# A Fourier filter and a swish layer on one core: the first batch multiplied from 94-row stationaries with one table, its rotations, filter loads and last stage rearranged, and four a1 buffers

## The chip, the core and the metric

The kernel runs on one core of a Trainium2 chip. The core has TensorE (PE, matrix products, with weight loads PEld), VectorE (DVE), ScalarE (ACT), GpSimd (POOL) and SyncE (SP, which here only issues DMAs). The metric is the device time of one execution in microseconds, as a median of runs.

## The reference

A batch of 8 sequences, 3008 tokens of 256 features, goes through a filter in the frequency domain and then through two matrices with a swish between them:

```python
X = np.fft.rfft(x, axis=1)
F = (filt_r + 1j * filt_i)[None, :, :]
y = np.fft.irfft(X * F, n=x.shape[1], axis=1)
h = y.reshape(B * S, D) @ w_in                    # 256 -> 2048
out = (h * (1.0 / (1.0 + np.exp(-beta * h)))) @ w_out   # 2048 -> 256
```

## The kernel before

**The transform.** 3008 = 47 x 64, so each transform is two products with small tables: s1 (47 points), s2 (64 points, with twiddles, table `t2`), the filter, and back through s3 (table `t3`, from `t2` by transposes) and s4 (table `t4`, from `t1` by a transpose). 24 groups of frequencies (`NK`) are treated; filters lie in `fr_sb` and `fi_sb`.

**Two ways through it.** Batches 1 to 7 use `s1`, `s2`, `s3`, `s4` (lines 545 to 624): s1 takes 94 rows of x (47 x 2) with the table `t1`, evicts into tiles `a1`, which `a1_store` writes to DRAM (line 344) and `a2_load` reads back turned (line 558); the same happens between s3 and s4 (`z`, `zz`). Batch 0 has nothing to hide behind, so it has functions of its own (`s1_0`, `s2_0`, `s3_0`, `z_turn`, `s4_0`), which turn with TensorE transposes instead of DRAM. Units of that work are six: three parts of eight groups (`KH` = 8), for each half of the 256 features.

**The main loop.** 752 steps (47 blocks of 512 tokens x 16 blocks of the hidden 2048). A step makes two products into `hps` (line 704), ScalarE's Silu into `gT` (line 713), then whatever `plan` holds for this step, and the four products into `acc` of the step two before (line 724); after 16 steps `acc` is evicted to `ost` and stored. Pieces of the next batches' transforms are put at chosen steps by `at`; for batch 1, s2 pieces are at steps 17, 20, ..., 50, each s3 five steps later, odd s3 and s4 pieces evicted by ScalarE.

**What sets the order.** The schedule is manual: each engine executes its instructions in the order in which the program writes them. An instruction that waits holds all behind it on its engine. GpSimd's queue also issues the loads with a cast (x, filters of the upper half, w_in), SyncE's the others. In the compiled program the DMAs of GpSimd use eight semaphores in turn, those of SyncE eight others; a DMA that comes to a semaphore again first waits for the landing of the DMA that had it.

**The first batch in order** (lines 131 to 531). x is loaded as 47 rows of 64 points (`x0`), in five pieces of two DMAs each. `s1_0(g)` makes sixteen products with the table `t1d` into a tile of two PSUM banks, evicted into `aT`; `spin` makes products that nobody uses. `t3_part(g)` makes a third of `t3` by eight transposes. `t3_rotate` makes `t3s`, a copy of `t3` with halves exchanged and signs changed, on VectorE (line 323); group 0 of it comes from `c10` by a transpose (line 329). `a0_turn` transposes eight groups of `aT` into `a0`. `s2_0(n)` makes the products of unit n and VectorE multiplies them by both filters (line 428, two instructions `pq_t`); `s3_0(n)` adds the products with `t3` and `t3s` into one tile, evicted to `zT`. `z_turn(e, hh)` transposes to `zz0`, and `s4_0(e, hh)` makes eight points of the result into a two-bank tile, evicted and scaled into `y`. The loop can begin when all of `y` is written.

**PSUM in the first batch.** `spsum` has three tiles of two banks (s1, s2, s3, s4), `tpsum` two tiles of one bank (all transposes and `spin`).

**Filters.** Each filter comes in three parts (`parts`: groups 0 to 8 and 8 to 24 of the first 128 features, then all groups of the second), one DMA per part from SyncE for the lower rows and one from GpSimd for the upper. GpSimd then copies each unit's rows to the other half of the partitions (`spread`, lines 460 and 461). Between the spreads it issues the loads of w_in and of batch 1's x (`load_x`). `reciprocal` and `scale_wout` (line 369) prepare w_out, scaled by 1/beta.

Of the kernel before, what the change touches and what calls it, by code (L numbers as in the profile page):

```python
# [10 lines left out]
P = 128  # L11

ACT = mybir.ActivationFunctionType
ALU = mybir.AluOpType
# [7 lines left out]
N1 = 47  # L22
# [14 lines left out]
def kernel(  # L37
# [38 lines left out]
    apool = ctx.enter_context(tc.tile_pool(name="apool", bufs=2))  # L76
# [7 lines left out]
    def load_filters(eng, k0, k1, d0, d1):  # L84
        lo = eng is nc.sync
        n = k1 - k0
        for filt, dst, p0 in ((filt_r, fr_sb, 0), (filt_i, fi_sb, M)):
            q0, off, sg = (p0, k0, 1) if lo else (p0 + H, N1 - k0, -1)
            src = AP(filt.tensor, filt.offset + off * D + d0, [[N1 * D, H], [sg * D, n], [1, d1 - d0]])
            eng.dma_start(dst[q0 : q0 + H, k0:k1, d0:d1], src)  # L90

    parts = ((0, KH, 0, E2), (KH, NK, 0, E2), (0, NK, E2, D))
# [42 lines left out]
    def turn8():  # L135
        return tpsum.tile([P, KH, P], BF16, name="tps", tag="tps")
# [7 lines left out]
    def fold(t):  # L144
        nc.vector.tensor_scalar(
            t, t, 32 - BITS, 32 - BITS, ALU.logical_shift_left, ALU.arith_shift_right
        )

    t1d = sp.tile([N1, 2 * NK], BF16, name="t1d", tag="t1d")
# [8 lines left out]
    aT = sr.tile([P, NDC, 2 * NK, M], BF16, name="aT", tag="aT")  # L158
# [4 lines left out]
    x0 = sq.tile([N1, M, D], BF16, name="x0", tag="x0")  # L163
    xv0 = x[0].rearrange("(n m) d -> n m d", m=M)
# [4 lines left out]
    def load_x0(m0, m1):  # L169
        nc.gpsimd.dma_start(x0[:32, m0:m1, :], xv0[:32, m0:m1, :])  # L170
        nc.gpsimd.dma_start(x0[32:, m0:m1, :], xv0[32:, m0:m1, :])

    load_x0(0, 16)
# [3 lines left out]
    load_x0(16, 32)  # L177
    iota(vi[:, :, :H], [[1, NK], [N1, H]])
    load_x0(32, 48)
    iota(vi[:, :, H:], [[1, NK], [-N1, H]], base=N1 * (M - 1))  # L180
    load_x0(48, 56)
    load_x0(56, 64)
    load_filters(nc.gpsimd, *parts[0])
    make_identity(nc, ident)
    with nc.allow_non_contiguous_dma(reason="2048 values, once"):
        nc.sync.dma_start(beta_sb[:], moe_beta.rearrange("(fb fp) -> fp fb", fp=P))
    seen = sp.tile([1, 2], BF16, name="seen", tag="seen")
    nc.sync.dma_start(seen[:], x0[:1, 16, :2])
    for part in parts:
        load_filters(nc.sync, *part)  # L190
    for part in parts[1:]:
        load_filters(nc.gpsimd, *part)
# [9 lines left out]
    def affine(name, src, mul, add):  # L202
        t = small(name)
        nc.vector.tensor_scalar(t[:], src[:], mul, add, ALU.mult, ALU.add)
        return t

    pn = affine("pn", ip, TURN / N1, 0.0)
    nc.vector.tensor_scalar_mul(cc[:], cc[:], TURN / 4)
    kcf, ccf = (t[:].rearrange("p a b -> p (a b)") for t in (kc, cc))

    def phase47(name, scale):
        t = sq.tile([P, 2 * NK], I32, name=name, tag=name)
        nc.vector.scalar_tensor_tensor(t[:], kcf, scale[:], ccf, ALU.mult, ALU.add)
        fold(t[:])
        return t

    ph_d = phase47("ph_d", pn)
    nc.scalar.activation(t1d[:], ph_d[:N1], ACT.Sin, scale=TWO_PI / TURN)
# [3 lines left out]
    off = affine("off", c_i, -TURN / 4, TURN / 4)  # L222

# [20 lines left out]
    MG = 8  # L244
    aTv = aT[:].rearrange("p e k (g m) -> p g e k m", m=MG)

    def s1_0(g, engines):
        ps = bank2([P, NDC, 512])
        for e in range(NDC):
            for i in range(MG):  # L250
                nc.tensor.matmul(
                    ps[:, e, i * 2 * NK : (i + 1) * 2 * NK],
                    lhsT=x0[:, g * MG + i, e * P : (e + 1) * P],
                    rhs=t1d[:],
                    start=True,
                    stop=True,
                )
        src = ps[:, :, : MG * 2 * NK].rearrange("p e (m k) -> p e k m", k=2 * NK)
        if len(engines) == 1:
            evac(aTv[:, g], src, engines[0])  # L260
        else:
            for e in range(NDC):
                evac(aTv[:, g, e], src[:, e], engines[e])

    def spin(m, n):
        ps = tpsum.tile([P, 512], F32, name="tps", tag="tps")
        for i in range(n):
            nc.tensor.matmul(
                ps[:, : 2 * NK], lhsT=x0[:, m + i % 16, :P], rhs=t1d[:], start=True, stop=True
            )  # L270

    def a0_turn(kg, e, on_act):
        tp = turn8()
        for kk_ in range(KH):
            k2 = 2 * (kg * KH + kk_)
            nc.tensor.transpose(
                tp[:, kk_, :], aT[:, e, k2 : k2 + 2, :].rearrange("p c m -> p (c m)"), ident[:]
            )
        evac(a0[:, kg * KH : (kg + 1) * KH, e * P : (e + 1) * P], tp[:], on_act)
# [6 lines left out]

    t2_half(0)
    t2_half(1)
    s1_0(0, (False,))
    s1_0(1, (True,))  # L290
    spin(0, 26)
# [3 lines left out]
    n1s = affine("n1s", shift_and("n1_i", 1, M - 1), TURN / N1, 0.0)  # L295
    ph_t = phase47("ph_t", n1s)
    sn = sq.tile([P, 2 * NK], F32, name="sn", tag="sn")
    nc.scalar.activation(sn[:], ph_t[:], ACT.Sin, scale=TWO_PI / TURN)
# [4 lines left out]
    q_i = shift_and("q_i", 0, 1)  # L303
    q_p = (affine("q0", q_i, -1.0, 1.0), affine("q1", q_i, 1.0, 0.0))
# [3 lines left out]
    c10 = sp.tile([P, P], BF16, name="c10", tag="c10")  # L308
    s1_0(4, (False,))
    s1_0(5, (True,))  # L310
    t3_part(1, True)
    for c in range(2):
        nc.vector.tensor_copy(c10[:, c * M : (c + 1) * M], t2[:, 0, (1 - c) * M : (2 - c) * M])
    t1v = t1[:].rearrange("p (k q) -> p k q", q=2)
    for q in range(2):
        nc.vector.tensor_scalar_mul(t1v[:, :, q], sn[:NP], q_p[q][:NP])
    s1_0(6, (False,))
    t3_part(2, True)
    s1_0(7, (True, False))

    def t3_rotate(k0, k1):
        for c in range(2):
            nc.vector.tensor_scalar_mul(
                t3s[:, k0:k1, c * M : (c + 1) * M], t3[:, k0:k1, (1 - c) * M : (2 - c) * M], rot[c][:]
            )

    t3_rotate(1, KH)
    tp0 = turn8()
    nc.tensor.transpose(tp0[:, 0, :], c10[:], ident[:])
    nc.scalar.activation(t3s[:, 0, :], tp0[:, 0, :], ACT.Copy, scale=sgn[:])  # L330
# [132 lines left out]
    units = [(0, 0), (1, 0), (2, 0), (0, 1), (1, 1), (2, 1)]  # L463
    for e in range(NDC):
        nc.gpsimd.memset(zT[e][:, WZ:], 0.0)
    spread(0)
    spread(1)
    nc.gpsimd.dma_start(win_sb[:], moe_w_in.rearrange("(dc p) f -> p dc f", p=P))
    spread(2)
    load_x(1, 0)  # L470
    spread(3)
    load_x(1, 1)
    spread(4)
# [6 lines left out]
    def turn_t4():  # L480
        tp = turn8()
        nc.tensor.transpose(tp[:KP, 0, :NP], t1[:], ident[:NP, :NP])
        nc.scalar.activation(t4[:], tp[:KP, 0, :NP], ACT.Copy)
        nc.gpsimd.tensor_scalar(t4[0:4], t4[0:4], 0.5, None, ALU.mult)

    s2_0(0)
    s2_0(1)
    t3_rotate(KH, NK)
    a0_turn(2, 0, True)
    s3_0(0)  # L490
    s2_0(2)
    a0_turn(0, 1, True)
    turn_t4()
    s3_0(1)
    s2_0(3)
    a0_turn(1, 1, False)
    s3_0(2)
    s2_0(4)
    a0_turn(2, 1, False)
    z_turn(0, 0, True)  # L500
    z_turn(0, 1, True)
    s3_0(3)
    s2_0(5)
    s4_0(0, 0, True)
    z_turn(0, 2, True)
    s4_0(0, 1, True)
    s3_0(4)
    z_turn(0, 3, True)
    s4_0(0, 2, True)
# [5 lines left out]
    nc.vector.reciprocal(rbeta_sb[:], beta_sb[:])  # L515
    scale_wout(0)
    scale_wout(WG)
    s3_0(5, True)
    s4_0(0, 3, True)
# [4 lines left out]
    z_turn(1, 3, True)  # L524
    s4_0(1, 1, True)
    s4_0(1, 2, False)
    s4_0(1, 3, True)
# [112 lines left out]
    def s23_steps(b, steps, lag, act):  # L640
        assert len(steps) == NU
        for i, s in enumerate(steps):
            at(s, s2, b, i)
            at(s + lag, s3, b, i, act and i % 2 == 1)

    def s4_steps(b, steps, act):
        assert len(steps) == J // 4 * NDC
        for i, s in enumerate(steps):
            at(s, s4, b, i, act and i % 2 == 1)

    for b in range(1, B):
        o = first_step[b - 1]
        if b == 1:
            s1_steps(1, range(16), [o + i // 2 for i in range(16)], False, range(1, 16, 2))
            for g in range(NG):
                at(o + 10, a2_load, 1, g)
            s23_steps(1, [o + 17 + 3 * i for i in range(NU)], 5, True)
            for h in range(J // JG):
                at(o + 59, zz_load, 1, h)
            s4_steps(1, [o + 67 + (i * 12) // 15 for i in range(16)], True)  # L660
            for f in (2, 3):
                at(f, load_wout, f * WG)
                at(f, scale_wout, f * WG)
            if B > 2:
                for g in range(4):
                    at(o + 14 + 3 * g, load_x, 2, g)
                late = (54, 55, 56, 57, 58, 59, 60, 61, 66, 67, 68, 70, 72, 73, 74, 76)
                s1_steps(2, range(16), [o + r for r in late], False)
                for g in range(NG):
                    at(o + 80, a2_load, 2, g)  # L670
                if B > 3:
                    for g in range(4):
                        at(o + (62, 68, 88, 92)[g], load_x, 3, g)
            continue
# [98 lines left out]
```

## Time and profile before

| | |
|---|---|
| median of 7 runs | 799.27 us (797.0 to 803.3) |
| the profiled execution | 799.4 us, of which the span of the core is 797.4 us |
| granted TensorE clock, mean | 0.996 |
| first product of `s1_0` | 6.77 us after the span's start |
| first product of `s2_0` (line 423) | 21.33 us |
| first and last product by a filter on VectorE (line 428) | 22.44 us, 41.11 us |
| DMA engines' mean busy share, 4 to 44 us | about 1 in nearly every 2 us; 0.2 and below from 44 to 54 us |
| costliest groups | 3008 `acc` products 453.5 us, 752 Silu 516.5 us, 1636 `hps` products 428.3 us |

All times in the text are microseconds from the start of the span. A row of the timeline gives start, duration, engine, line, operation, output and inputs with their shape, how many instructions were merged, and in brackets the idle time of the engine before it and what ended it. A line can be that of a helper: line 112 is an eviction by ScalarE and lines 114 and 116 by VectorE, so that one goes by the names of the tiles. The kernel after has other line numbers.

### The profile page before, as it was taken

How to read it: one execution, taken by the hardware profiler on the slowest of the kernel's cores; microseconds unless marked ns; L12 is line 12 of the kernel's file. 1: busy time of each engine (PE TensorE's matmuls, PEld its weight loads, DVE VectorE, ACT ScalarE, POOL GpSimd, SP SyncE). 2: the span in 40 equal slices, each digit the busy share in tenths (PEclk: the TensorE clock that was granted, in tenths of full speed). 3: DMA queues.
4: the chain of work that ended last, by engine and by line, in shares of the span. 5: the costliest groups of instructions: out<-in, count | busy, mean ns of one | idle time of the engine just before them, and what ended most of it. 6: DMA issues, size and time to landing. Idle time of an engine off the chain costs nothing.

```text
span 797.4 us, 15328 instructions
## 1 busy us (share of the span) xinstructions
PE 765.1 (96%) x6040; PEld 549.2 (69%) x6132; DVE 443.7 (56%) x694; ACT 555.5 (70%) x813; POOL 170.5 (21%) x191
## 2 busy tenths in 40 slices
PE   5688999999999999999999999999999999999997
PEld 4665666766677666776668766786667766676665
DVE  6753875476556675567655666556754666330100
ACT  5486777766667666676667666677766777777776
POOL 7824431132202321023211312011210122000000
PEclk9999999999999999999999999999999999999999
DMA  9947538542762319413383134903244211500101
GB/s 149 227 119 195 113 85 220 132 113 66 170 180 74 86 53 231 140 47 86 92 225 106 59 101 113 255 28 97 63 140 152 68 52 47 152 28 27 54 27 53
DMA packets 87163, 88.29 MB, mean 111 GB/s; under 512 B 6017, under 2 KB 78209, under 8 KB 86951
## 3 DMA queue, kind: packets, MB, share of 16 engines
q1 hardware_dynamic: 82356, 72.37, 30.7%
q0 software_dynamic: 4736, 14.95, 11.6%
q8 instruction: 48, 0.79, 0.4%
q14 instruction: 23, 0.19, 0.1%
HBM read 54.01 MB, written 46.66 MB: 126 GB/s over the span
## 4 chain that ended last, share of the span: by engine, by line
PE 90%; DMA 2%; ACT 1%; DVE 1%; issue 1%; ACTq 0%; SPq 0%; DVEq 0%
PE acc L724 41%; PE hps L704 37%; PE ps L550 3%; PE ps L617 3%; PE ps L595 3%; PE ps L566 2%; DMA d<-a 1%; DMA a<-d 1%; ACT gT L713 0%; ACT a L112 0%; DVE ost L114 0%; DVE y L116 0%; ACT y L112 0%; ACT zz L112 0%; ACT zT L112 0%
## 5 line engine op out<-in xcount | busy, mean ns | idle before, releaser
L713 ACT ACTIVATE gT<-hps,beta_sb 128x512 bf16<-128x512 f32 x752 | 516.5, 687 | 213.8 <-PE hps L704 193.1
L724 PE MATMUL acc<-wout_sb,gT 128*128 128x256 bf16 x3008 | 453.5, 272 | 4.9 <-DVE ost L114 2.6
L704 PE MATMUL hps<-y,win_sb 128*128 128x512 bf16 (+7 forms) x1636 | 428.3, 350 | 0.8 <-DVE y L116 0.5
L724 PEld LDWEIGHTS <-gT 128*128 128x128 bf16 x3008 | 287.5, 98 | 129.8 <-issue 6.3
L585 POOL TENSOR_TENSOR yh<-a_t,b_t 128x512 bf16<-128x512 f32 x84 | 106.3, 1265 | 422.7 <-DVE b_t L584 415.8
L704 PEld LDWEIGHTS <-win_sb 128*128 128x128 bf16 x1728 | 164.9, 98 | 24.9 <-issue 0.8
L114 DVE COPY ost<-acc 128x512 f32<-128x512 f32 x93 | 59.9, 686 | 137.4 <-PE acc L724 137.3
L580 DVE TENSOR_TENSOR a_t<-ps,fr_sb 128x512 f32<-128x512 f32 x84 | 58.1, 692 | 82.0 <-PE ps L566 81.4
L114 DVE CAST a<-ps 96x512 bf16<-96x512 f32 x104 | 70.7, 685 | 51.5 <-PE ps L550 46.4
L116 DVE TENSOR_SCALAR y<-ps 128x376 bf16<-128x376 f32 x104 | 56.0, 548 | 59.4 <-PE ps L617 59.1
L581 DVE SCALAR_TENSOR_TENSOR b_t<-ps,fi_sb 64x512 f32<-64x512 f32 x84 | 58.2, 693 | 1.1
L584 DVE TENSOR_TENSOR b_t<-ps,fi_sb 64x512 f32<-64x512 f32 x84 | 57.4, 684 | 1.1
L114 DVE CAST z<-ps 128x512 bf16<-128x512 f32 x78 | 53.4, 685 | 1.8 <-PE ps L595 0.8
L617 PEld LDWEIGHTS <-zz 96*128 96x128 bf16 x448 | 29.8, 98 | 22.9
L550 PE MATMUL ps<-xg,t 94*96 94x512 bf16 x112 | 41.8, 381 | 2.3 <-ACT a L112 1.8
L617 PE MATMUL ps<-t,zz 96*128 96x94 bf16 x448 | 34.7, 205 | 0.8
L595 PE MATMUL ps<-yh,t 128*128 128x256 bf16 x168 | 32.1, 273 | 0.6
L566 PE MATMUL ps<-a,t 128*128 128x256 bf16 x168 | 32.1, 273 | 0.6 <-DMA a<-d 0.3
L595 PEld LDWEIGHTS <-t 128*128 128x128 bf16 x168 | 16.2, 98 | 17.7
L356 POOL DMA_DIRECT2D xg<-in_x_dram x28 | 15.3, 545 | 59.3 <-PE ps L550 59.3
L566 PEld LDWEIGHTS <-t 128*128 128x128 bf16 x168 | 16.1, 98 | 16.8 <-DMA a<-d 0.6
L550 PEld LDWEIGHTS <-t 94*96 94x96 bf16 x112 | 13.8, 123 | 10.5 <-issue 0.3
(99 smaller groups left out, 201.3 us busy)
## 6 DMA issues: line engine op xcount, KB each, us to landing
out_dram<-ost SPq DMA_DIRECT2D x46, 512.0 KB, 3.0
d<-a SPq DMA_DIRECT2D x28, 384.0 KB, 4.5
a<-d SPq DMA_DIRECT2D x28, 384.0 KB, 5.2
d<-z SPq DMA_DIRECT2D x28, 384.0 KB, 3.8
zz<-d SPq DMA_DIRECT2D x28, 384.0 KB, 6.8
xg<-in_x_dram POOLq DMA_DIRECT2D x28, 320.0 KB, 5.7
ws<-in_moe_w_out_dram SPq DMA_DIRECT2D x4, 512.0 KB, 6.2
xg<-in_x_dram POOLq DMA_DIRECT2D x28, 56.0 KB, 5.6
```

Of the source, the lines that this page charges most:

```text
L114: nc.vector.tensor_copy(dst, src)
L550: nc.tensor.matmul(ps[:KP], lhsT=t1[:], rhs=xg[b, g][:, jj : jj + 2, :], start=True, stop=True)
L566: nc.tensor.matmul(ps[:, e, :], lhsT=t2[:, k0 + e, :], rhs=st["a2", b, g][:, kk + e, :], start=True, stop=True,)
L580: nc.vector.tensor_tensor(a_t[:], ps[:], fr_sb[:, ks, :], ALU.mult)
L581: nc.vector.scalar_tensor_tensor(b_t[:M], ps[M:], -1.0, fi_sb[M:, ks, :], ALU.mult, ALU.mult)
L584: nc.vector.tensor_tensor(b_t[M:], ps[:M], fi_sb[M:, ks, :], ALU.mult)
L585: nc.gpsimd.tensor_tensor(yh[:], a_t[:], b_t[:], ALU.add)
L595: nc.tensor.matmul(ps[:, e, :], lhsT=t3[:, 2 * i + e, :], rhs=yh[:, e, :], start=True, stop=True)
L617: nc.tensor.matmul(ps[:, e, :NP], lhsT=zz[:, j0 % JG + e, dc * P : (dc + 1) * P], rhs=t4[:], start=True, stop=True,)
L704: nc.tensor.matmul(hps[:, pos - t0 : pos - t0 + ln], lhsT=win_sb[:, dc, fb * P : (fb + 1) * P], rhs=ys[b][:, dc, n0 : n0 + ln], start=(dc ...
L713: nc.scalar.activation(gT[:], hps[:], ACT.Silu, scale=beta_sb[:, fb : fb + 1])
L724: nc.tensor.matmul(acc[tb // 2][:, tb % 2, :], lhsT=gT[:, tb * P : (tb + 1) * P], rhs=wout_sb[:, fb, :], start=(fb == 0 and tb % 2 == 0), ...
```

## The change

All but items 1 and 7 concerns the first batch.

1. `apool` (tiles `a1`) has four buffers instead of two.
2. x is loaded as 94 rows of 32 points (80 + 14 rows a piece, five pieces of the same bytes), and `s1_0(g)` makes eight products of 96 columns with `t1`, the table of the other batches; `t1d` and its Sin go. Per piece half as many products, twice the columns; evictions have as many elements, with the inner run of 4 instead of 8. `spin` makes 3 products of 512 columns instead of 26 of 48.
3. The filters come in five parts (one per unit for the first four units, then one for two units), so ten DMAs on each queue instead of six. On GpSimd all are issued ahead of the spreads and after the last pieces of x, the identity ahead of those pieces, and filt_i ahead of filt_r.
4. `turn_t4` (with its small operation on GpSimd) comes after `t3_part(0)`; `t3_part(2)` and the turn of `c10` come after `s2_0(0)`; the second part of `t3_rotate` is split in two and goes to ScalarE, as do two evictions of `a0_turn`, and between `s2_0(0)` and `s3_0(5)` VectorE has the filter products only.
5. For the first 128 features the last stage is `f_0`: four points into a one-bank tile of `tpsum`, eight times, in place of `s4_0`, eight points into a two-bank tile of `spsum`, four times.
6. The load of w_in comes one spread later; `reciprocal` and both `scale_wout` move to just before the last two `s4_0`; the memsets of `zT` move behind the load of w_in.
7. In the loop, for batch 1: s2 pieces at steps 18, 21, 23, 26, 28, 30, 34, 36, 39, 41, 44, 46; s3 still five later, all evicted by ScalarE; the loads of `zz` at step 56 instead of 59.

```diff
-    apool = ctx.enter_context(tc.tile_pool(name="apool", bufs=2))
+    apool = ctx.enter_context(tc.tile_pool(name="apool", bufs=4))
...
-    parts = ((0, KH, 0, E2), (KH, NK, 0, E2), (0, NK, E2, D))
+    parts = ((0, KH, 0, E2), (KH, 2 * KH, 0, E2), (2 * KH, NK, 0, E2), (0, KH, E2, D), (KH, NK, E2, D))
...
-    x0 = sq.tile([N1, M, D], BF16, name="x0", tag="x0")
-    xv0 = x[0].rearrange("(n m) d -> n m d", m=M)
+    x0 = sq.tile([NP, J, D], BF16, name="x0", tag="x0")
+    xv0 = x[0].rearrange("(p j) d -> p j d", j=J)
...
-    MG = 8
+    MG = 4
...
                 nc.tensor.matmul(
-                    ps[:, e, i * 2 * NK : (i + 1) * 2 * NK],
+                    ps[:, e, i * KP : (i + 1) * KP],
                     lhsT=x0[:, g * MG + i, e * P : (e + 1) * P],
-                    rhs=t1d[:],
+                    rhs=t1[:],
...
+    def f_0(e, u, on_act):
+        ps = tpsum.tile([P, 4, P], F32, name="tps", tag="tps")
+        for i in range(4):
+            nc.tensor.matmul(
+                ps[:, i, :NP],
+                lhsT=zz0[:, 4 * u + i, e * P : (e + 1) * P],
+                rhs=t4[:],
+                start=True,
+                stop=True,
+            )
+        dst = ys[0][:, e, :].rearrange("p (n j) -> p n j", j=J)
+        evac(
+            dst[:, :, 4 * u : 4 * u + 4],
+            ps[:, :, :NP].rearrange("p j n -> p n j"),
+            on_act,
+            inv_scale,
+        )
+
+    spread(0)
+    spread(1)
+    spread(2)
+    nc.gpsimd.dma_start(win_sb[:], moe_w_in.rearrange("(dc p) f -> p dc f", p=P))
     for e in range(NDC):
         nc.gpsimd.memset(zT[e][:, WZ:], 0.0)
-    spread(0)
-    spread(1)
-    nc.gpsimd.dma_start(win_sb[:], moe_w_in.rearrange("(dc p) f -> p dc f", p=P))
-    spread(2)
+    spread(3)
     load_x(1, 0)
-    spread(3)
+    spread(4)
     load_x(1, 1)
-    spread(4)
     spread(5)
...
     s2_0(0)
+    t3_part(2, True)
+    tp0 = turn8()
+    nc.tensor.transpose(tp0[:, 0, :], c10[:], ident[:])
+    nc.scalar.activation(t3s[:, 0, :], tp0[:, 0, :], ACT.Copy, scale=sgn[:])
     s2_0(1)
-    t3_rotate(KH, NK)
     a0_turn(2, 0, True)
+    t3_rotate(KH, 2 * KH, True)
     s3_0(0)
     s2_0(2)
     a0_turn(0, 1, True)
-    turn_t4()
+    t3_rotate(2 * KH, NK, True)
     s3_0(1)
     s2_0(3)
-    a0_turn(1, 1, False)
+    a0_turn(1, 1, True)
     s3_0(2)
     s2_0(4)
-    a0_turn(2, 1, False)
+    a0_turn(2, 1, True)
     z_turn(0, 0, True)
     z_turn(0, 1, True)
+    f_0(0, 0, True)
+    f_0(0, 1, True)
     s3_0(3)
     s2_0(5)
-    s4_0(0, 0, True)
     z_turn(0, 2, True)
-    s4_0(0, 1, True)
+    f_0(0, 2, True)
+    f_0(0, 3, True)
+    z_turn(0, 3, True)
     s3_0(4)
-    z_turn(0, 3, True)
-    s4_0(0, 2, True)
+    f_0(0, 4, True)
...
+    f_0(0, 5, True)
     s3_0(5, True)
-    s4_0(0, 3, True)
+    f_0(0, 6, False)
+    f_0(0, 7, True)
     z_turn(1, 0, False)
     z_turn(1, 1, True)
     s4_0(1, 0, False)
     z_turn(1, 2, False)
-    z_turn(1, 3, True)
     s4_0(1, 1, True)
-    s4_0(1, 2, False)
-    s4_0(1, 3, True)
+    z_turn(1, 3, False)
+    nc.vector.reciprocal(rbeta_sb[:], beta_sb[:])
+    scale_wout(0)
+    scale_wout(WG)
+    s4_0(1, 2, True)
+    s4_0(1, 3, False)
...
-            s23_steps(1, [o + 17 + 3 * i for i in range(NU)], 5, True)
+            s23_steps(1, [o + r for r in (18, 21, 23, 26, 28, 30, 34, 36, 39, 41, 44, 46)], 5, 1)
             for h in range(J // JG):
-                at(o + 59, zz_load, 1, h)
-            s4_steps(1, [o + 67 + (i * 12) // 15 for i in range(16)], True)
+                at(o + 56, zz_load, 1, h)
+            s4_steps(1, [o + 67 + (i * 12) // 15 for i in range(16)], 2)
```

## The prediction

> **What bounds the kernel now.** I read the page first, then busy time in three windows, then TensorE in order of time.
>
> ```profile
> span 797.4 us, 15328 instructions
> PE 765.1 (96%) x6040; PEld 549.2 (69%) x6132; DVE 443.7 (56%) x694; ACT 555.5 (70%) x813; POOL 170.5 (21%) x191
> ```
>
> TensorE sets the time; the question is where its missing 32 us lie. The windows are cut at the first `hps` matmul (50.99) and after the last larger gap (92); the columns are busy time and instructions of each engine, clock, DMA share, GB/s.
>
> ```profile
> 0.00:50.99 50.99, 32.86 (x500) 29.48 (x501) 35.30 (x63) 29.05 (x38) 35.87 (x57) 0.97 0.90 165
> 50.99:92.00 41.01, 36.11 (x236) 23.84 (x241) 21.47 (x32) 28.67 (x46) 15.22 (x16) 1.00 0.68 163
> 92.00:797.40 705.40, 696.14 (x5306) 495.86 (x5390) 386.90 (x600) 497.73 (x730) 119.38 (x119) 1.00 0.38 104
> ```
>
> No engine is full in the first window: it is a chain of waits, 51 us long, and all of it counts, since from its end TensorE runs without a break. After 92 us TensorE is at 98.7%, and the edits leave its work there as it is. Between lie five gaps, which these rows of TensorE's timeline show (last bracket: idle time and who ended it):
>
> ```profile
> 50.99 0.73 PE L704 MATMUL hps<-y,win_sb 128*128 128x512 bf16 x2 [0.53 <-DVE y L116]
> 57.92 0.38 PE L550 MATMUL ps<-xg,t 94*96 94x512 bf16 x1 [0.26 <-ACT a L112]
> 62.18 0.38 PE L550 MATMUL ps<-xg,t 94*96 94x512 bf16 x1 [1.49 <-ACT a L112]
> 71.33 0.39 PE L566 MATMUL ps<-a,t 128*128 128x256 bf16 x2 [0.31 <-DMA a<-d]
> 74.63 0.38 PE L724 MATMUL acc<-wout_sb,gT 128*128 128x256 bf16 x2 [1.82 <-DVE ost L114]
> 91.68 0.38 PE L724 MATMUL acc<-wout_sb,gT 128*128 128x256 bf16 x2 [0.81 <-DVE ost L114]
> ```
>
> So a change in the first batch can win in two places: at 50.99, and in gaps of 0.26+1.49+0.31+1.82+0.81 = 4.69 us.
>
> **First stage: the 94-row products.** 128 matmuls of 48 columns become 64 of 96. These rows say what that is worth:
>
> ```profile
> 10.66 1.44 PE L251 MATMUL sps<-t1d,x 47*128 47x48 bf16 x32 [1.41 <-DMA x<-in_x_dram]
> 16.27 1.04 PE L284 MATMUL tps<-ident,t 128*128 128x128 bf16 x8
> 38.37 0.61 PE L437 MATMUL sps<-t,pq_t 128*128 128x128 bf16 x8
> ```
>
> Less a tail of about 0.17 us, 48 columns cost 40 ns and 128 columns 107 ns: time goes by columns, at half the pace of the third row (55 ns). So 64 x 80 = 128 x 40 = 5.1 us: nothing is won on TensorE itself. A rule bears on this half pace. The Trainium skill (TensorE: Matmul & The Clock Gate, "What's actually happening") has the array at full clock after some 3.4 us of sustained work; here it is busy nearly without a break from 10.66 to 18.3 and the transposes at 16.27 are still at half pace; the quick ones begin at 23.81. By the rule the new stage would be quick from about 14, and everything before the loop would end 1.8 us earlier than in my sum; by the rows it stays slow to about 23.8. I take the rows and keep the 1.8 us for the low end.
>
> The first product now waits for the one table: Sin 0.24, then two multiplies on VectorE behind half a `t2` (0.68 + 0.56) and perhaps behind an iota on GpSimd: 8.1 instead of 6.77. This costs nothing: the second piece of x lands only at 10.66, and x's bytes are the same. Its pieces landed at 6.6, 10.5, 13.1, 14.3 and 15.4; the same is taken for 94 rows, since the later `xg` loads have that form and are no slower. If they come later, each us costs 1 us. The evictions keep 768 elements with inner runs of 4, not 8: `y` rows with runs of 4 (376 elements, 548 ns) and of 8 (752, 942 ns) differ as their sizes do, so nothing for that.
>
> What counts is what leaves TensorE's queue ahead of `a0_turn(0,0)`: `t3_part(2)` (0.85) and the `c10` transpose go behind `s2_0(0)`; only the table's transpose (0.1) comes in. The queue then runs s1 to 16.2, `t3_part(1)` to 17.1, `a0_turn(0,0)` from 17.1 (18.81 before), and `s2_0(0)` at 19.25, after VectorE's rotate (2 x 0.73, ending 18.3) and eviction (0.68). Before, it was 21.33. First product: 20.6 against 22.44, 1.9 us won.
>
> **Middle: VectorE, filters, ScalarE.** VectorE loses the rotate of groups 8 to 24 (1.93) and two a0 evictions (0.68 each): 3.3 us. Its twelve products are then 12 x 1.13 = 13.6 us (a row of 1.22 repeats every 1.13). They can't run at that pace, for three reasons in turn:
>
> Filters. These rows give the landing times of the pieces of before:
>
> ```profile
> fi_sb<-in_filt_i_dram POOLq DMA_DIRECT2D x1, 128.0 KB, 6.7
> fi_sb<-in_filt_i_dram POOLq DMA_DIRECT2D x1, 256.0 KB, 11.3
> fi_sb<-in_filt_i_dram SPq DMA_DIRECT2D x1, 384.0 KB, 18.2
> ```
>
> Issued at 10.81, 13.33 and 12.85, they landed at 17.5, 24.6 and 31.1. The bytes are the same and the DMA share is full from 4 to 44 us, so I put the new pieces on that line: unit 0 at 17.8, 1 at 21.2, 2 at 24.6, 3 at 26.1, units 4 and 5 at 29 to 31.1. Each queue issues four DMAs more, 0.65 us each on GpSimd, 0.5 on SyncE. In the compiled order each queue's DMAs use eight semaphores in turn, so the last pair on GpSimd waits for the landing of its first filter pair (about 17.5); t4's halving (0.48) and all spreads stand behind it. Spread 0 starts at 19.5 (18.42 before). The layout bears a start up to 20.6 and landings up to 1.2 us later at no cost, beyond that 1 us per us; the w_out loads behind SyncE's queue are not due before 46. win_sb and the memsets, moved past one spread, stay due near 40, ahead of the loop.
>
> GpSimd: two copies of 1.08 a unit, and 1.09 of xg issue after unit 3 and after unit 4, put spread 5 at 34.3 and 35.3.
>
> ScalarE is the later one. It receives four rotates (about 0.60 each, from the 512-element eviction's 604 ns) and two more a0 evictions (1.02), and eight `f_0` evictions, one of them on VectorE (376 elements, 475 ns) stand for four of 796. From 19.5 to 42.0 it has fifteen of 0.92, four of 0.50, seven of 0.37 and 0.8 of small ones = 19.2 us in 22.5. TensorE's order makes that the path: transposes and `f_0` share two PSUM tiles, so `z_turn(0,1)`, `f_0(0,0)` and `f_0(0,1)` each wait for ScalarE to give one back, and `s3_0(3)` with `s2_0(5)` stand behind them.
>
> The resulting starts, before and after: `s3_0(3)` 38.37, 34.2; `s2_0(5)` 39.26, 35.1; last product's end 42.33, 38.2; `s3_0(5)` 44.06, 39.6; `z_turn(1,0)` 45.91, 42.0; last `y` ends 50.94, 47.6. One us of the lead is lost at the end, where `f_0(0,6)` and `(0,7)` hold the tiles that `z_turn(1,*)` needs. The same addition over the kernel before gives 51.25 where the trace has 50.99, so I take 0.26 off: the loop starts at 47.35, 3.6 us earlier.
>
> The reciprocal moves to about 46.0. Behind it GpSimd scales w_out (1.89 each), done at 47.9 and 49.8; TensorE wants the first 2.8 us into the loop, about 50.2. Hidden, with 2 us to spare; without that cover it would cost up to 1.9.
>
> **In the loop.** Four a1 buffers: the first s1 evictions no longer wait for stores, so 0.26+1.49 go. What is late next is the fourth store: evicted at loop +10.4, issued +10.5, landed 3.05 later as before, then a2 5.0 later: +18.6. `s2` is now at step 18 instead of 17: 18.28 of unstalled TensorE time plus 0.87 = +19.15. The 0.31 goes, with half a us of margin. The 1.82 and 0.81 arose because the three product rows of `s2` (0.69 each) of steps 17 and 32 stood before `ost` on VectorE; the new steps 18, 30 and 34 leave it free at steps 17 and 33. All z evictions on ScalarE add 0.48 in a step: 0.57+0.48 = 1.05 under TensorE's 1.09 with s3. I take 4.4 of the 4.69, leaving 0.3 for a tight slot; bounds 3.0 and 4.7.
>
> **Sum.** The profiled execution took 799.4 us, of which 2.0 lie outside its span; the median shown is 799.27, no different. 799.4 - 3.6 - 4.4 = 791.4.
>
> **Rivals.** (a) ScalarE eats the first part: if its extra work (2.4 of rotates, 2.0 of a0) is all on the path and PSUM waits add to it, the loop starts at 51 as before and only the gaps go: 795.0. For it, ScalarE's 85%; against, it had 12 us idle there. (b) The clock is up early, the rule's case: 789.6. (c) The gaps move: the 94-row part wins 3.6, but a2 lands after step 18 or z evictions hold gT: 2 to 3 us come back, 794. (d) Slower: GpSimd stands at the issue of its ninth filter piece until the first has landed, and spread 0 behind it. It costs 1 us per us from a start of 20.6, and outweighs the 8 us from 28.6; the first piece would have to take some 16 us where that row shows 6.7 and the longest 18.2. With 30 it would be 801. A rule for it: the Trainium skill (DMA: Bandwidth & Descriptors, "Anatomy of one DMA") gives about 2.0 us fixed per DMA, so four more in a row would be 8 us. But rows of 128 KB landed in 6 to 7 us while five others were in flight: fixed parts overlap here. By the row 0, by the rule fi lands at 39, 1.2 of it free: 798.2. (e) The edits cancel: no change.
>
> **Chances.** Main 0.64 (789.8 to 793); a 0.12; b 0.07; c 0.07; d 0.06 (its lighter half lands near 798); e 0.04. The range, 788.8 to 795.6, takes in a, b and c and leaves out d, e and 1 in 10 of the main case. A measurement here can tell about 0.3%, 2.4 us: faster 0.90 (main, a, b, c), same 0.07 (e, half of d), slower 0.03.
>
> **What would show it.** First `hps` at 47 to 48; `s2_0(0)` near 19.3; spread 0 near 19.5; ScalarE above 80% busy from 20 to 42; no gap over 0.3 us between the first `hps` and step 50, `s2` at loop +19 not ended by a DMA. Wrong: spread 0 after 20.6, x pieces later than 15.4, a gap at `acc` ended by `ost`, or 8 transposes at 0.61 before 20.

## The result, and the profile after

The changed kernel takes 791.02 us (median of 12 runs, 789.58 to 794.68) where the kernel before, run beside it, takes 798.64 (31 runs). The ratio is 0.9909, 95% interval 0.9896 to 0.9923: 0.9% faster, some 7.3 us. Forecast were 791.4 us and 788.8 to 795.6.

The profiled execution took 794.68 us and is the slowest of the twelve. That has to be kept in mind with every row below; the reason is found further on. One execution of all (e1's traced one, below) took 4597.54 us, with TensorE slow from end to end, and stands in no comparison. First the page's head, then busy time in three windows cut as before, at the first `hps` (47.60) and 705.4 us ahead of the end (87.50):

```profile
span 792.9 us, 15158 instructions
PE 764.8 (96%) x5953; PEld 547.8 (69%) x6045; DVE 437.0 (55%) x683; ACT 562.4 (71%) x826; POOL 172.9 (22%) x195
```

```profile
0.00:47.60 47.60, 31.43 (x413) 27.54 (x414) 32.59 (x58) 32.77 (x45) 35.76 (x60) 1.00 0.90 176
47.60:87.50 39.90, 37.31 (x238) 24.68 (x243) 20.35 (x30) 29.49 (x48) 17.91 (x18) 0.96 0.69 168
87.50:792.90 705.40, 696.06 (x5305) 495.60 (x5389) 384.08 (x596) 500.14 (x734) 119.22 (x118) 1.00 0.38 104
```

The last window is cut to be as long as before. It also holds the same work (5305 matmul records for 5306, 696.06 us for 696.14), so all of the 4.5 us between the two spans lies in the first two: 3.39 in the first batch (50.99 to 47.60), and only 1.11 in the second window, where 4.4 were forecast. TensorE's timeline of the changed kernel shows why. These rows stand where the five gaps stood:

```profile
47.60 0.59 PE L719 MATMUL hps<-y,win_sb 128*128 128x512 bf16 x2 [1.03 <-DVE y L117]
...
68.83 0.38 PE L581 MATMUL ps<-a,t 128*128 128x256 bf16 x2 [2.33 <-DMA a<-d]
69.04 0.60 PE L739 MATMUL acc<-wout_sb,gT 128*128 128x256 bf16 x4
69.48 0.81 PE L719 MATMUL hps<-y,win_sb 128*128 128x512 bf16 x2
70.08 1.06 PE L739 MATMUL acc<-wout_sb,gT 128*128 128x256 bf16 x4
70.94 1.06 PE L719 MATMUL hps<-y,win_sb 128*128 128x512 bf16 x2
71.79 1.06 PE L739 MATMUL acc<-wout_sb,gT 128*128 128x256 bf16 x4
72.64 0.84 PE L719 MATMUL hps<-y,win_sb 128*128 128x512 bf16 x2
73.32 0.38 PE L581 MATMUL ps<-a,t 128*128 128x256 bf16 x2
```

Both waits for `a` and both for `ost` are gone. The wait for a2, 0.31 before, has grown to 2.33, and behind it the same groups of matmuls take 1.06 in place of 0.60: about 3.4 us at which the array works at half its pace. From the first `s2` to the second it is 4.49 us; the same instructions take 2.82 in an execution without the half pace (g2 below), so that costs 1.67. Added up: 3.39 + 4.69 - 2.33 - 1.67 = 4.08 of 4.5; where the other 0.4 was won is not known.

Who is late is to be seen on two queues of the changed kernel, GpSimd's and SyncE's (start, duration):

```profile
60.67 0.60 POOL L351 DMA_DIRECT2D xg<-in_x_dram  x1
61.28 0.52 POOL L352 DMA_DIRECT2D xg<-in_x_dram  x1
61.79 0.53 POOL L351 DMA_DIRECT2D xg<-in_x_dram  x1
62.31 0.52 POOL L352 DMA_DIRECT2D xg<-in_x_dram  x1
```

```profile
55.25 2.88 SPq L339 DMA_DIRECT2D d<-a  x2
62.17 5.53 SPq L573 DMA_DIRECT2D a<-d  x4
```

Two loads of batch 2's x are issued from 60.67 on, 1.5 us ahead of the a2 loads, while the last store of a1 is still under way. That store landed 4.4 us after its issue (forecast 3.05), the first a2 load, for which `s2` waits, in 6.6 (forecast 5.0), and the median of the four in 7.6. In the kernel before only one x load went ahead (64.70); the second stood on GpSimd behind the `yh` of an `s2` of step 17 and came at 75.16. In the new plan nothing of `s2` is at step 17, so it goes too. The prediction followed every queue in the first batch and did not look at GpSimd's here.

### The profile page after: what moved, and what is told of

Its sections match the earlier page's. It is cut to its first block, busy times and chain, and to the rows that moved or that the text cites. A ratio compares the mean times of both kernels' runs of the same rounds, so it can differ in the third digit from the quotient of the medians.

```text
span 792.9 us, 15158 instructions
## 1 busy us (share of the span) xinstructions
PE 764.8 (96%) x5953; PEld 547.8 (69%) x6045; DVE 437.0 (55%) x683; ACT 562.4 (71%) x826; POOL 172.9 (22%) x195
## 4 chain that ended last, share of the span: by engine, by line
PE 93%; ACT 2%; DMA 2%; POOL 1%; issue 1%; DVE 1%; POOLq 0%; ACTq 0%
PE acc L739 42%; PE hps L719 38%; PE ps L565 3%; PE ps L632 3%; PE ps L610 3%; PE ps L581 2%; DMA a<-d 1%; DMA x<-in_x_dram 1%; ACT zz L113 0%; ACT a L113 0%; ACT zT L113 0%; POOL x L170 0%; ACT t3s L288 0%; POOL x L171 0%; DVE y L117 0%
## 5 line engine op out<-in xcount | busy, mean ns | idle before, releaser
L115 DVE CAST z<-ps 128x512 bf16<-128x512 f32 x72 | 49.3, 685 | 1.7 <-PE ps L610 0.8
L565 PE MATMUL ps<-xg,t 94*96 94x512 bf16 x112 | 41.5, 381 | 0.6
```

Of the source, the lines that this page charges most:

```text
L115: nc.vector.tensor_copy(dst, src)
L565: nc.tensor.matmul(ps[:KP], lhsT=t1[:], rhs=xg[b, g][:, jj : jj + 2, :], start=True, stop=True)
```

## The experiments

"Before" is timed beside each group of four: 798.55, 799.07 and 799.2 us. Ratios are to before.

**The wait for a2.** e1 moves the loads of batch 2's x alone:

```diff
-                    at(o + 14 + 3 * g, load_x, 2, g)
+                    at(o + 20 + 3 * g, load_x, 2, g)
```

> The changed kernel with batch 2's four x loads at steps 20, 23, 26 and 29 instead of 14, 17, 20 and 23, so that none of them is in flight while a2 is read. Theory (the 2.33 us gap at step 18 is a2 landing late because two x loads of batch 2 were issued at 60.7 and 61.8, just ahead of the a2 loads at 62.2): the a2 landing comes back to 5 us after issue and the fourth store to 3 us, so the gap falls below 0.5 us, the half pace after it goes, and the median falls by 1 to 3 us, to 788 to 790. Rival (the chain of four stores and four a2 loads is too long by itself): the gap stays at 2 us or more and the time at 791.

Measured: 790.34 us, 0.9895 [0.9881, 0.9909], from three executions of 789.7 to 790.55, none of them traced. So the same edit was run again (g2), beside the changed kernel itself (g1):

> The changed kernel with the loads of batch 2's x six steps later (from step 20 in place of 14), so that GpSimd issues at most one of them ahead of the a2 loads. If these loads are why a2 lands late, the first s2 of the loop waits for a2 less than 0.5 us (2.33 in the changed kernel's trace), the a2 loads land in 5 to 6 us (6.6 to 7.6), and the time is 0.5 to 3 us below the changed kernel's in this job. If the stores or the early start of the loop are why, the wait stays at 1.5 us or more, and the time is the same within 0.5 us.

> The changed kernel once more, unaltered, beside the others of this job. If what costs time after the first hps (a wait for a2 of 2.33 us and about 3 us at half pace behind it) belongs to the kernel, this trace has them again, and the median is 790 to 792. If they belong to the one execution that was traced, the wait is under 0.5 us here, and the time of this execution is 2 to 3 us below the other's 794.9.

Measured: g2 788.9 us (788.77 to 791.39), 0.9879 [0.9857, 0.9901]; g1 791.95 us (789.91 to 796.73), 0.9910 [0.9884, 0.9937]. TensorE, SyncE and GpSimd of g2:

```profile
45.84 0.59 PE L719 MATMUL hps<-y,win_sb 128*128 128x512 bf16 x2 [1.03 <-DVE y L117]
...
64.58 0.38 PE L581 MATMUL ps<-a,t 128*128 128x256 bf16 x2
...
67.40 0.38 PE L581 MATMUL ps<-a,t 128*128 128x256 bf16 x2
```

```profile
53.49 2.88 SPq L339 DMA_DIRECT2D d<-a  x2
59.54 2.16 SPq L573 DMA_DIRECT2D a<-d  x4
```

```profile
68.87 0.60 POOL L351 DMA_DIRECT2D xg<-in_x_dram  x1
```

With the x loads out of the way (first one at 68.87) the last store landed after 3.3 us, the four issues of a2 took 2.16 us in place of 5.53, the loads landed in 4.9 (median), and `s2` starts 18.74 us after the first `hps` without a wait: what was forecast of the changed kernel (+19.15). In g1, the changed kernel once more, the wait is there again, with the x loads at 61.71 and a2 at 63.03:

```profile
70.89 0.38 PE L581 MATMUL ps<-a,t 128*128 128x256 bf16 x2 [3.55 <-DMA a<-d]
71.11 0.67 PE L739 MATMUL acc<-wout_sb,gT 128*128 128x256 bf16 x4
71.58 1.06 PE L719 MATMUL hps<-y,win_sb 128*128 128x512 bf16 x2
...
74.14 0.99 PE L739 MATMUL acc<-wout_sb,gT 128*128 128x256 bf16 x4
```

Of the changed kernel's 18 executions (with g1's) seven took more than 792 us; of the eight of e1 and g2 (without the one left out above) none did. That the wait is in the two traced ones of the seven is shown; that it is in the other five is only likely.

e2 leaves the loads and gives a2 three steps more:

```diff
-            s23_steps(1, [o + r for r in (18, 21, 23, 26, 28, 30, 34, 36, 39, 41, 44, 46)], 5, 1)
+            s23_steps(1, [o + r for r in (21, 23, 26, 28, 30, 34, 36, 39, 41, 44, 46, 50)], 5, 1)
-                at(o + 56, zz_load, 1, h)
+                at(o + 59, zz_load, 1, h)
```

> The changed kernel with the s2 pieces of batch 1 at steps 21, 23, 26, 28, 30, 34, 36, 39, 41, 44, 46, 50 (zz loads at step 59 as in the kernel before), so that TensorE has three more steps of its own work before it needs a2. Both theories of the late a2 expect the gap at the first s2 product to vanish (2.6 us of extra work against 2.33): median 788 to 790. If instead a new gap of over 0.5 us appears at ost, z or zz, the tighter end of the plan takes the gain back: 790.5 to 792.

Measured: 791.47 us (789.34 to 791.92), 0.9901 [0.9885, 0.9918]. There is no gap over 0.16 us after the first `hps` (47.89) until 132. Here three x loads were issued beside a2, which was slower than ever (issues of 7.0 us, landing in 10.9), and the later step hid it. No execution is over 792 here either, but the median is no lower than the changed kernel's.

**The two parts of the loop, each alone on the kernel before.** e3 has the four a1 buffers only (its diff follows), e4 only the new steps of item 7, with all z evictions on ScalarE:

```diff
-    apool = ctx.enter_context(tc.tile_pool(name="apool", bufs=2))
+    apool = ctx.enter_context(tc.tile_pool(name="apool", bufs=4))
```

> The kernel before with four a1 buffers and nothing else. Theory (the two gaps of 0.26 and 1.49 us are waits for a1 stores and go, while the a2 landing moves up with the fourth store, since only one x load is in flight): 796.9, the gap at a2 below 0.6 us. Rival (the DMA chain sets the first s2, the buffers only move the wait): 798.6 as before, the gap at a2 grows to about 2 us.

> The kernel before with the new steps of batch 1 alone (s2 at 18, 21, ..., all z evictions by ScalarE, zz at 56). Theory: the gaps of 1.82 and 0.81 us at ost go; the second x load of batch 2, no longer held behind the first yh on GpSimd, is issued ahead of a2 and makes that gap about 1 us instead of 0.31: 796.7. Rival (the steps cost nothing elsewhere): 796.0. If ost still ends a gap of over 0.5 us, the reading of these gaps was wrong.

Measured: e3 797.71 us, 0.9992 [0.9981, 1.0003]; e4 798.59 us, 0.9998 [0.9984, 1.0013]. TensorE of e3 keeps only the two waits for `ost`:

```profile
72.08 0.38 PE L724 MATMUL acc<-wout_sb,gT 128*128 128x256 bf16 x2 [1.89 <-DVE ost L114]
...
89.11 0.38 PE L724 MATMUL acc<-wout_sb,gT 128*128 128x256 bf16 x2 [0.80 <-DVE ost L114]
```

TensorE of e4 has lost those two and has the new one:

```profile
60.55 0.38 PE L550 MATMUL ps<-xg,t 94*96 94x512 bf16 x1 [1.20 <-ACT a L112]
...
72.70 0.39 PE L566 MATMUL ps<-a,t 128*128 128x256 bf16 x2 [2.21 <-DMA a<-d]
```

Each edit removes the gaps that the prediction gave to it. The new steps bring the wait for a2 on the kernel before as well, with two x loads 1.5 us ahead of the a2 loads (first x load at 63.13, a2 at 64.65): of the 2.63 won at `ost` 1.90 are given back in this trace, and the median does not move. That e3's median gains only 0.8 us where its trace lacks 2.06 of gaps stays unexplained.

**The first stage.** f1 gives the kernel before the 94-row products and their one table, with all else in its old order (its diff has the rows of `x0`, `aT`, `MG`, and `t1` in place of `t1d`, as in the change).

> The kernel before with the 94-row stationaries and the one table alone; the order of everything behind s1, the filter parts, the evictions and the last stage stay as they were. If TensorE's time goes by columns at half pace (64 products of 80 ns for 128 of 40 ns), nothing is won: s1 ends at about 16 to 17 us, first hps between 50.0 and 51.2, time 798 to 799. If fewer products matter by themselves (half as many instructions and weight loads), s2_0(0) starts 1 us or more earlier than 21.33 and the first hps follows: below 49.8, time 796.5 to 797.5. If the one table that is now waited for costs on the path, first hps above 51.5 and time above 799.5.

Measured: 799.32 us, 1.0000 [0.9982, 1.0017]. Nothing is won by them, as the sum 64 x 80 = 128 x 40 had it; the first `hps` at 50.08 is within what the kernel before varies by (50.70 and 49.60 in e3 and e4, whose first batch is the old one).

**Who does what between 20 and 42.** f2 takes both later rotates and two a0 evictions back to VectorE:

```diff
-    t3_rotate(KH, 2 * KH, True)
+    t3_rotate(KH, 2 * KH, False)
...
-    t3_rotate(2 * KH, NK, True)
+    t3_rotate(2 * KH, NK, False)
...
-    a0_turn(1, 1, True)
+    a0_turn(1, 1, False)
...
-    a0_turn(2, 1, True)
+    a0_turn(2, 1, False)
```

> The changed kernel with the two later t3 rotates and the evictions a0_turn(1,1) and a0_turn(2,1) on VectorE again, so that VectorE has not only products and ScalarE has 3.5 to 4 us less. If ScalarE is the path between 20 and 42 us (my working), the relief is worth up to 2 us, if VectorE's 12 products (1.13 each) with 3.9 us more of rotates and evictions still keep up with GpSimd's spreads, and first hps falls at 46 to 47.5 and the time is 789 to 791. If the products on VectorE are the path, first hps moves out by 2 to 3.5 us, to 49.5 to 51, and the time is 793 to 794.5. If neither (the spreads on GpSimd set it), first hps stays at 47.6 within 0.5.

Measured: 796.56 us, 0.9971 [0.9955, 0.9987], first `hps` with all of `y` at 52.99. This one part is worth some 5 us, more than the whole gain of the first batch. VectorE's timeline of f2:

```profile
26.08 1.32 DVE L290 TENSOR_SCALAR t3s<-t,rot 128x512 bf16<-128x512 bf16 x2
27.33 1.21 DVE L423 TENSOR_TENSOR pq_t<-sps,fr_sb 128x1024 bf16<-128x1024 f32 x1
28.46 1.21 DVE L423 TENSOR_TENSOR pq_t<-sps,fi_sb 128x1024 bf16<-128x1024 f32 x1
29.59 0.96 DVE L290 TENSOR_SCALAR t3s<-t,rot 128x512 bf16<-128x512 bf16 x2
...
36.44 0.68 DVE L115 COPY a<-tps 128x1024 bf16<-128x1024 bf16 x1
40.91 1.22 DVE L423 TENSOR_TENSOR pq_t<-sps,fr_sb 128x1024 bf16<-128x1024 f32 x1 [3.79 <-issue]
```

VectorE is not full (15.9 of 22 us from 20 to 42; ScalarE falls to 11.0). It is order that costs: each rotate stands in the queue ahead of a product, TensorE waits for `t3s` (1.16 and 0.82) and for `a` (2.25), and the last pair of products starts at 40.91 in place of 35.91. Behind these waits the array also fell to half pace (rows of 1.06 from 38.91 to 41.5, in the changed kernel 0.61), which cost some 1.4 of the 5 us: from `s3_0(3)` to `z_turn(0,3)` it is 4.89 us in place of 3.45. So the moved work loads ScalarE, but taking it off ScalarE that way does not help.

f4 brings back the three filter parts:

```diff
-    parts = ((0, KH, 0, E2), (KH, 2 * KH, 0, E2), (2 * KH, NK, 0, E2), (0, KH, E2, D), (KH, NK, E2, D))
+    parts = ((0, KH, 0, E2), (KH, NK, 0, E2), (0, NK, E2, D))
```

> The changed kernel with the filters in three parts per queue as before: 4 DMAs fewer on each queue, so GpSimd does not stand at its ninth and tenth filter issue, and spread 0 can start when the first part has landed. If the pieces per unit are worth what the order of landings says (unit 1 at 21.2 in place of 24.6), spread 1 waits for a filter here, spread 0 starts at 18.5 to 19.5, unit 1 at 24.5 or later, unit 5 after 31, and first hps moves out by 1 to 2 us, time 792 to 793. If the stand at the ninth issue was the larger cost, first hps comes at 46.5 to 47.3 and time is 789.5 to 790.7. If ScalarE sets the path whatever the filters do, no change within 0.4 us.

Measured: 792.0 us (790.23 to 795.6), 0.9907 [0.9878, 0.9937]: no different. GpSimd's timeline of f4, above, and of the changed kernel, below:

```profile
17.88 1.03 POOL L455 COPY fr_sb<-fr_sb 64x1024 f32<-64x1024 f32 x1 [2.78 <-issue]
...
22.46 1.04 POOL L455 COPY fr_sb<-fr_sb 64x1024 f32<-64x1024 f32 x1 [2.45 <-DMA fr_sb<-in_filt_r_dram]
```

```profile
17.09 0.68 POOL L91 DMA_DIRECT2D fi_sb<-in_filt_i_dram  x1 [0.72 <-DMA fi_sb<-in_filt_i_dram]
19.05 0.65 POOL L91 DMA_DIRECT2D fr_sb<-in_filt_r_dram  x1 [1.29 <-DMA fr_sb<-in_filt_r_dram]
...
20.27 1.03 POOL L455 COPY fr_sb<-fr_sb 64x1024 f32<-64x1024 f32 x1
```

Both expected effects are there: without the stand at the ninth and tenth issue spread 0 starts 2.4 us earlier, then spread 1 waits 2.45 for its filter. Spread 5 starts at 34.91 (34.22). That they cancel is true of the medians. The traces differ also in the array's pace, quick in f4 from 15.24 (eight transposes in 0.61), slow in the changed kernel until 22. Beside g2, which has the five parts and was quick as well, f4 starts the loop 0.7 us later (46.57 against 45.84), so the five parts are worth something there, less than six executions can show.

f3 puts the first half's last stage back into four two-bank tiles of the other pool, in the old order:

```diff
-    f_0(0, 0, True)
-    f_0(0, 1, True)
     s3_0(3)
     s2_0(5)
+    s4_0(0, 0, True)
...
```

> The changed kernel with the last stage of the first half in four two-bank tiles again (s4_0 on the other PSUM pool) in place of eight one-bank tiles that share the transposes' tiles. If the shared tiles are what holds z_turn and the products behind them (my working put the path there), or if ScalarE's longer evictions of 796 ns weigh little, first hps moves to 46.5 to 47.6 and the time is 790 to 791. If the pieces are worth something by starting earlier and filling gaps, first hps moves out by 0.5 to 1.5 us, time 791.5 to 792.5.

Measured: 788.84 us (787.65 to 790.24), 0.9865 [0.984, 0.989], whose interval lies below that of the changed kernel. Its trace has no wait for a2 (first x load at 58.11, a2 at 58.20), so not all of this need come from the tiles; what they do is seen beside g2, which has no such wait either. TensorE of f3, and of g2, which has the pieces and ran its first stages equally quick:

```profile
30.84 0.61 PE L432 MATMUL sps<-t,pq_t 128*128 128x128 bf16 x8
...
31.74 0.61 PE L418 MATMUL sps<-a,t 128*128 128x128 bf16 x8
```

```profile
32.38 0.33 PE L462 MATMUL tps<-t,zz 96*128 96x94 bf16 x4 [0.57 <-ACT zz L113]
32.55 0.61 PE L432 MATMUL sps<-t,pq_t 128*128 128x128 bf16 x8
...
33.44 0.61 PE L418 MATMUL sps<-a,t 128*128 128x128 bf16 x8
```

`s3_0(3)` and `s2_0(5)` start 1.7 us earlier where `f_0` does not wait for the transposes' tiles ahead of them; of that 1.3 reach the loop (first `s2` 63.27 against 64.58). So the one-bank pieces lose in the traces; the medians of f3 and g2 (788.84, 788.9) do not tell the two apart.

**The array's pace.** g4 keeps TensorE busy from the start:

```diff
+    hot = sp.tile([P, 512], BF16, name="hot", tag="hot")
+    nc.vector.memset(hot[:], 0.0)
...
+    ps_hot = tpsum.tile([P, 512], F32, name="tps", tag="tps")
+    for _ in range(16):
+        nc.tensor.matmul(ps_hot[:], lhsT=hot[:, :P], rhs=hot[:], start=True, stop=True)
     t2_half(0)
```

> The changed kernel with 16 added matmuls of 512 columns on a tile of zeros (not part of the computation, nothing reads them) ahead of the first s1, so that TensorE is busy from about 1.5 us and the array is at full pace well before 12. If the pace of the array up to 22 us holds the chain (the rival of an early clock, 1.8 us), s2_0(0) starts 1 to 1.5 us before 19.3, first product and first hps move by the same, and the time is 1.2 to 1.8 us below the changed kernel's in this job. If GpSimd's spreads set the first product, s2_0(0) starts earlier but the first product stays at 21.0 to 21.4, first hps moves by less than 0.5, and the time is the same within 0.7 us.

Measured: 790.67 us (789.91 to 793.75), 0.9899 [0.9877, 0.9922], first `hps` at 46.93. It did not do what it was made for. Two windows of g4 follow; the third number from the end is the granted clock, 0.58 and 0.50:

```profile
12.00:16.00 4.00, 2.83 (x41) 2.55 (x39) 2.80 (x9) 2.43 (x4) 3.09 (x6) 0.58 1.00 225
16.00:19.00 3.00, 2.67 (x26) 2.38 (x25) 1.76 (x4) 1.40 (x2) 0.92 (x2) 0.50 1.13 224
```

The transposes at 11.76 were quick (0.61 where the changed kernel has 1.01), but from 12 to 19 the array was at half pace again, and `s2_0(0)` came at 19.04. So the run is inconclusive on what a lastingly quick array would give; g2 answers that, as its array happened to be quick.

**All together.** g3 is f3 with the later x loads and the later `s2`:

> The changed kernel with the first half's last stage in four two-bank tiles, the x loads of batch 2 from step 20, and the products of s2 from step 21 in place of 18: the version that the experiments point to. If the three gains stand beside each other, first hps starts at 44 to 46, no gap over 0.3 us is left before step 50, and the time is 786.5 to 788.5, below both kernels. If the big tiles' 2 us come from an execution whose array was quick early, the time is 789.5 to 791 as without them.

Measured: 789.12 us (787.16 to 790.13), 0.9875 [0.9849, 0.9901]. Its trace is the shortest of all (span 785.2, no gap over 0.2 from step 1 to step 50), but f3, g2 and g3 are one by their medians, 788.8 to 789.1. They beat the kernel before by 1.2 to 1.35%, the changed one by some 2 to 3 us; g2's and g3's intervals still overlap with that of g1 beside them.

## Why the prediction was right, and the step that failed

**The first batch held.** `s2_0(0)` 19.32 (forecast 19.25), `s3_0(3)` 34.31 (34.2), `s2_0(5)` 35.21 (35.1), last product's end 38.26 (38.2), `s3_0(5)` 39.64 (39.6), `z_turn(1,0)` 41.94 (42.0), first `hps` 47.60 (47.35). Spread 0 came at 20.27 for 19.5, just under the 20.6 from which it costs, because the tenth filter issue waited too; the first product at 21.33 for 20.6. A rotate takes 0.67 to 0.72 for 0.60. Both were mis-sized by little and hidden: in e2 spread 0 started at 19.45, and the loop no earlier (47.89). The rotates and evictions moved off VectorE carry the 3.4 us (f2: without them it is lost), the products alone give nothing (f1), the filter pieces at most 0.7 (f4), the one-bank pieces lose some 1.3 (f3): the prediction named that wait for the two tiles, and counted it as inevitable. The new order of `t3_part(2)` and the other turns (rest of item 4) and item 6 were not undone alone.

**ScalarE became the path, and does not eat the gain.** It is busy 19.61 of the 22 us from 20 to 42 (10.38 before). ScalarE of the changed kernel has no pause in these rows:

```profile
23.00 1.02 ACT L113 ACTIVATE a<-tps 128x1024 bf16<-128x1024 bf16 x1 [0.43 <-PE tps L272]
23.92 1.33 ACT L288 ACTIVATE t3s<-t,rot 128x512 bf16<-128x512 bf16 x2
25.14 1.01 ACT L113 ACTIVATE zT<-sps 128x1024 bf16<-128x1024 f32 x1
26.05 1.02 ACT L113 ACTIVATE a<-tps 128x1024 bf16<-128x1024 bf16 x1
```

The chain of waits followed back from the end of that trace lies wholly on ScalarE from 23.00 to 30.12 and changes between it and TensorE until 39.5; the products on VectorE are not in it. In four executions with the same evictions the first `hps` follows the start of the `a0_turn(2,0)` eviction by 24.60 (changed), 24.61 (e2), 24.71 (g2) and 24.88 us (g4), although they started between 21.13 and 23.28. In g1, where the array fell to half pace at 33.7, it is 26.04.

**The clock was no rival but a matter of the execution.** In the traced one the array is slow until 22, as the rows of before had it; in g2, with the same first batch, `s2_0(0)` takes 0.61 in place of 1.06. The changed kernel and g2:

```profile
19.32 1.06 PE L418 MATMUL sps<-a,t 128*128 128x128 bf16 x8
```

```profile
18.29 0.61 PE L418 MATMUL sps<-a,t 128*128 128x128 bf16 x8
```

The loop of g2 starts 1.76 us earlier, where the working put 1.8 on a quick array. The filters also landed sooner in g2 (spread 0 at 19.23), but so they did in e2 (19.45), which had the slow array and started the loop at 47.89; so the filters did not do it. Of the 1.76 at most 0.4 is x's last piece, which landed sooner in g2 (its products start at 15.26 in place of 15.64); the rest is the pace. The prediction had named eight transposes at 0.61 before 20 as a sign of being wrong: g1 and g2 have them, the traced execution has not. Rule and row each held, in different executions. The rule has a second half that I did not weigh: the Trainium skill (TensorE: Matmul & The Clock Gate, "What's actually happening") says that the window in which activity is judged runs freely, some 3.4 us long, so that the turning point differs from run to run of one kernel, by half a us either way. These traces agree that it differs, but by far more: the transposes of groups 8 to 15, near 16 us, take 1.05, 0.61, 0.61 and 1.05 us in the changed kernel, g1, g2 and g4; the changed kernel is quick only from 22.35, and g1 was slow once more from 18.14 (1.01) to 19.80. What decides it in one execution stays open.

**The step that failed:** "The 0.31 goes, with half a us of margin." It did not; a wait of 2.33 came, and with it 1.67 of half pace. The term that was wrong is the a2 landing, "landed 3.05 later as before, then a2 5.0 later": both durations were taken from a trace in which one x load went ahead of them, and the new plan moves a second one there. In the changed kernel they took 4.37 and 6.61, which is 2.93 more and uses up the half us of margin; `s2` came at loop +21.23, held by a DMA, in place of +19.15. Rival (c), "a2 lands after step 18", with "2 to 3 us come back, 794", is what the traced execution shows, at 794.68. In the traces the wait goes roughly with how far the x loads lead: two loads leading a2's issue by 1.50, 1.32, 1.52 and 1.00 us go with waits of 2.33 (changed), 3.55 (g1), 2.21 (e4) and 1.38 (f4); leads of 0.18 and 0.09 with 0.78 (f2) and none (g4 and f3). One load leading by 2.12, 1.58 and 0.03 goes with 1.34 (f1), 0.31 (before) and none (e3). The lead is not the whole of it: it grows when the last store is late, which an x load can cause, and in e2, with a lead of 0.54, a2 took longest. That the x loads are the cause rests on g2, which moved them and nothing else.

The executions can be put together from these terms, with g2's 788.77 (`hps` 45.84, no wait) as base. Changed kernel: 788.77 + 1.76 + 2.33 + 1.67 = 794.53, measured 794.68. g1: 788.77 + 2.61 + 3.55 + 1.68 = 796.61, measured 796.73. By the same terms a slow first batch without the wait gives 790.5, which is the case that was forecast at 791.4. The trace of e2 is such a case: the terms give a span of 789.05 and it has 789.1; its 791.47 us hold 2.4 us outside the span where g2's hold 1.8. As far as the traces go, the wait puts an execution above the forecast case, and a quick array without the wait puts it below; how many of the eighteen were of which kind is not known. So part of the number's closeness is luck: the wait, which I had excluded, and the quick array, which I had not counted on, stand on either side of it.

## What to carry to other kernels

When a plan of steps is shifted, list what every queue issues in the shifted stretch, not only the engine that waited: here a load of the next batch had been held back by a product of the old step, by nobody's intent. A landing time from a trace holds only with the neighbours it had; before using it as a due time, ask which transfers the change puts beside it. And undo the parts one by one even where the whole is a gain: of the four parts of the first batch that were undone, one carried it, two moved no median, and one cost 1.3 us in the trace. Compare traces only where the array's pace was the same; between two executions of one first batch up to 1.8 us of difference came from it.

## What the runs showed of the hardware

A pause of TensorE can be paid for twice: after 2.33 and 3.55 us of waiting the array ran 3.4 us at half pace (1.67 more), in e4 after 2.21 us it did not. It also fell to half pace after pauses of 0.57 us (g1 at 33.7) and 1.03 us (f4 at 47.4, where the stretch up to the first `s2`, 18.7 us in g2, took 20.5 without the wait); the same pauses cost nothing in g2. The length of the last pause alone does not decide it. The granted clock of a window shows it in some cases (0.59 in the changed kernel from 69 to 73) and not in others: in the changed kernel it stands at 1.00 from 16 to 19, where eight transposes take 1.05 us. The duration of equal rows is the surer sign.
